# A two-stage Fourier mix on one core: the middle channel joined to channel 0, and the even-cosine product split by output parity

## The chip, the core and the metric

The kernel runs on one core of one Trainium2 chip. A core has five engines with a queue each: TensorE (PE; PEld are its weight loads), VectorE (DVE), ScalarE (ACT), GpSimd (POOL) and SyncE (SP, which here issues nearly all DMAs). Each works its own queue in order and waits on semaphores for the others. The metric is the time on the device in microseconds (us); lower is better.

## The reference

```python
# attention, for each of 8 batches and 8 heads; q, k, v are (8, 8, 576, 64), fp32
q_s = exp(q - max(q, -1)); q_s /= sum(q_s, -1) + 1e-9
k_s = exp(k - max(k, seq)); k_s /= sum(k_s, seq) + 1e-9
x = q_s @ (k_s.T @ v)                       # then (batch, 576, 8 * 64 = 512)

# Fourier mix and a two-layer MLP, for each batch
mixed = real(fft(fft(x, axis=1), axis=2))   # over 576 tokens, then over 512 channels
u = x + mixed
un = (u - mean(u, -1)) / sqrt(var(u, -1) + 1e-6)
out = u + relu(un @ w_ch1) @ w_ch2          # 512 x 2048 and 2048 x 512
```

## The kernel before

**Batches and order.** The eight batches follow each other, each in stages: attention, first Fourier stage (over tokens), second Fourier stage (over channels), normalisation, and the MLP's two layers (`up` and `down`, whose products are formed by Strassen's scheme; for batch 2 and later `down` goes two levels deep). The work is written as a list of steps with times, sorted by them once; each engine's queue is the order in which the steps issue. So attention and Fourier work of the next batch stand among the MLP products of the present one, at places fixed by hand. Batch 0 has an order of its own (`OPENING`); batch 1 is mixed into batch 0's plain MLP; batches 2 to 7 come from `timed`. The 64 tokens of a batch that don't fill a tile of 128 are shared: two batches form one tile together (`g`, and `mix_shared`).

**First Fourier stage.** The input is real, so only cosines and sines of folded inputs are needed. `folded` adds and subtracts mirrored tokens (`tokens_folded`), then mirrored channels (`columns_folded`, L1110), then token halves (`by_frequency`, L1123), and folds the channels once more (`columns_again`, L1129 and L1130): for each of four tiles `eo[i]`, L1129 writes the difference of mirrored channels and L1130, in place, their sum. They go over the tiles in the order 2, 3, 0, 1; tiles 2 and 3 feed the sines, 0 and 1 the cosines. `folds` (L1085 to L1088) does the same for the shared tokens' tile `g`. The order on DVE is that of the code: for tile 0 L1129, L1130, for tile 1 L1129, L1130, and then sums for the deep `down` (L1617). On POOL stand, at about the same time in batches 2 to 7, four sums of the last hidden tile (`a_side`, L405 to L408).

The products then take the tiles as stationary operands: five groups of channels k, each with an odd and an even half of the tokens (`blocks`, L1207): sines 2 and 3, then cosines 0, 1 and 4. Group 4 is one channel alone, the middle channel (number 128, `QD`) of the twice folded 128 (it is computed as 128 wide, of which one row is used). `tails` (L1234) adds the shared tokens. In batch 1 `block` (L1166, L1169) does the same, one group at a time. `copies` then lays the results out in SBUF by ACT: group k to `Z[:, k]` (L1246, "own") and, for the 64 shared rows, to `ZT[:, k]` (L1249, L1250); group 4 goes to row 0 of the tiles `Zr` and `ZTr`, whose other rows were set to zero at the start.

**Second Fourier stage.** `second` forms for each tile of 128 tokens one row of 512 outputs in PSUM: odd cosines from group 1, even cosines from group 0 (129 columns), sines from 2 and 3 (all on L1264). The middle channel's cosine is +1 for outputs of even number and -1 for odd ones; it is added to the even cosines by a product of its own (L1267), with `Zr` as 128 rows of which one is not zero and a row of signs as moving operand. ACT copies the sines (L1273), DVE forms sums and differences (L1281), and they are added to x. There are 20 such mixes: two own tiles in each of eight batches, and four shared ones.

All products are fp32; the profile lists each as two matmul records with a weight load each.

Of the kernel before, what the change touches and what calls it, by code (L numbers as in the profile page):

```python
# [43 lines left out]
ALU = mybir.AluOpType  # L44
AX = mybir.AxisListType

P = 128
B, H, S, DH = 8, 8, 576, 64
D = H * DH
# [9 lines left out]
Q = 32  # L59
# [79 lines left out]
class _Block:  # L139
# [906 lines left out]
    def t_times_kv(self, b):  # L1046
        nc, V = self.nc, self.nc.vector
        j, box = b % 2, []
        part = slice(W * j, W * j + W)

        F = lambda r: self.F[:, 2 * r + j]

        def times():
            box.extend(self.by_head(b, F, False, DH, shared=b != 1))
            px = box[-1]
            for a in range(2):
                for h in range(2):
                    for i in range(2):
                        n = HD + a * DH if b < 2 else FREE + (1 + a) * DH
                        t = box[2 + h] if b == 1 else px[-1][:, h]  # L1060
                        nc.tensor.matmul(t[64 * i:64 * i + 64, n:n + DH], lhsT=F(2 * i + a)[64 * h:64 * h + 64, P:],
                                         rhs=self.pairs[j][64 * h:64 * h + 64, 2 * i + a, 0:DH], start=True, stop=True)

        def copies():
            g = self.live["g", b] = self.halves()
            x = self.xshared(b // 2)[part]
            if b != 1:
                px = box.pop()
                for r, t in box:
# [12 lines left out]

        def folds():
            g = self.live["g", b]
            V.scalar_tensor_tensor(out=g[:, 1:HD], in0=g[:, D - 1:HD:-1], scalar=self.sign[:, 0:1], in1=g[:, 1:HD],  # L1085
                                   op0=ALU.mult, op1=ALU.add)
            V.tensor_tensor(out=g[:, NN:NN + QD], in0=g[:, 0:QD], in1=g[:, HD:QD:-1], op=ALU.subtract)
            V.tensor_tensor(out=g[:, 0:QD], in0=g[:, 0:QD], in1=g[:, HD:QD:-1], op=ALU.add)  # L1088

        return [(0, times), (1.3, copies), (8 if b > 1 else 3, folds)]  # L1090

    def folded(self, b):
# [30 lines left out]
        def columns_again(some):  # L1125

            for i in some:
                t, y = eo[i], eo[i][:, NN:]
                V.tensor_tensor(out=t[:, 0:QD], in0=y[:, 0:QD], in1=y[:, HD:QD:-1], op=ALU.subtract)  # L1129
                V.tensor_tensor(out=y[:, 0:QD], in0=y[:, 0:QD], in1=y[:, HD:QD:-1], op=ALU.add)  # L1130

        if b == 0:
            return tokens_folded, lambda some: (columns_parted if some[0] < 2 else columns_folded)(some), by_frequency, columns_again
# [12 lines left out]
    def block(self, b, k):  # L1146
        nc = self.nc
        box = []
        sines = k in (2, 3)
        own = slice(*{0: (NN, NN + QD), 4: (NN + QD, NN + QD + 1), 1: (0, QD), 2: (NN + 1, NN + QD + 1),  # L1150
                      3: (1, QD)}[k])
        tail = slice(*{0: (0, QD), 4: (QD, QD + 1), 1: (NN, NN + QD), 2: (1, QD + 1), 3: (NN + 1, NN + QD)}[k])
        n = own.stop - own.start
        if k == KT:

            own, tail = slice(own.start, own.start + P), slice(tail.start, tail.start + P)

        def times():
            eo, g = self.eo[b], self.live["g", b]
            if b not in self.Z:  # L1160
                self.Z[b] = self.work.tile([P, KT, HD], F32, tag="Z", name="Z", bufs=1)
            full = self.acc((own.stop - own.start, 512))
            f = sines * NM
            for odd, at, size in ((1, 0, MO), (0, MO, ME)):
                t = eo[3 - odd if sines else odd]
                nc.tensor.matmul(full[:, at:at + size], lhsT=t[:, own], rhs=self.ft[:, f + at:f + at + size], start=at == 0,  # L1166
                                 stop=False, skip_group_check=True)
            f += 2 * NM
            nc.tensor.matmul(full[:, 0:NM], lhsT=g[:, tail], rhs=self.ft[:, f:f + NM], start=False, stop=True,  # L1169
                             skip_group_check=True)  # L1170
            box.append(full[0:n])

        def copies():
            pz, Z = box.pop(), self.Z[b]
            z, zt = (self.Zr[0:1], self.ZTr[0:1]) if k == KT else (Z[0:n, k, :], self.ZT[0:n, k, :])
            nc.scalar.copy(paired(z), interleaved(pz[:, NT - 1:NT - 1 + 2 * ME])[:, 0:P, :])

            at = W * (b % 2)
            nc.scalar.mul(paired(zt[:, at:at + Q]), interleaved(pz[:, 0:2 * MO])[:, 0:NT - 1, ::-1],
                          -1.0 if sines else 1.0)  # L1180
            nc.scalar.copy(paired(zt[:, at + Q:at + W]), interleaved(pz[:, 0:2 * ME])[:, NT - 2::-1, ::-1])

        return [(0, times), (1.4, copies)]

    def blocks(self, b):

        nc = self.nc
        box = {}
        eo = self.eo.setdefault(b, {})
        cols = {0: (NN, 0), 1: (0, NN), 2: (NN + 1, 1), 3: (1, NN + 1), 4: (NN + QD, QD)}  # L1190
        wide = lambda k, i: slice(cols[k][i], cols[k][i] + (QD - 1 if k == 3 else P))
        place = lambda k, odd: slice((0, 1, 0, 1, 2)[k] * (ME - odd), (0, 1, 0, 1, 2)[k] * (ME - odd) + ME - odd)
        bank = lambda k, odd: box[k in (2, 3)][:QD - 1 if k == 3 else P, 1 - odd, place(k, odd)]
# [41 lines left out]
                                     start=first.get(k, False), stop=True, skip_group_check=True)  # L1235

        def copies(k, part, copy=nc.scalar.copy):
            n, sines, Z = {3: QD - 1, 4: 1}.get(k, P), k in (2, 3), self.Z[b]
            z, zt = (self.Zr[0:1], self.ZTr[0:1]) if k == KT else (Z[0:n, k, :], self.ZT[0:n, k, :])
            flat = box[sines][0:n].rearrange("p a n -> p (a n)")  # L1240
            odd, even = place(k, 1).start, D + place(k, 0).start

            def both(x, y, size, step=1):
                return bass.AP(flat.tensor, flat.offset + x, [flat.ap[0], [step, size], [y - x, 2]])
            if part == "own":
                copy(paired(z), both(odd + NT - 1, even + NT, P))  # L1246
                return
            w = W * (b % 2)
            nc.scalar.mul(paired(zt[:, w:w + Q]), both(even, odd, NT - 1), -1.0 if sines else 1.0)  # L1249
            nc.scalar.copy(paired(zt[:, w + Q:w + W]), both(even + NT - 1, odd + NT - 2, NT - 1, -1))  # L1250

        return own, tails, copies, early, sine

    def second(self, z, zr, adds, two=True, apart=None):

        nc, V = self.nc, self.nc.vector
        cd, box = self.cd, []
# [1 line left out]
        def times():  # L1259
            banks = apart() if apart else [self.acc((P, D), two)] * 2  # L1260
            parts = (1, 0, QD), (0, QD, QD + 1), (2, NN + QD - 1, QD), (3, NN, QD - 1)
            for k, at, size in (parts[2], (3, HD, QD), *parts[:2]) if apart else parts:
                rows, pm = QD - 1 if k == 3 else P, banks[k > 1]
                nc.tensor.matmul(pm[:, at:at + size], lhsT=z(k)[0:rows], rhs=cd[0:rows, at:at + size], start=True,  # L1264
                                 stop=(k != 0))
                if k == 0:
                    nc.tensor.matmul(pm[:, at:at + size], lhsT=zr(), rhs=cd[:, D:], start=False, stop=True)  # L1267
            box.extend(banks)

        def copy():  # L1270
# [30 lines left out]
    def mix_own(self, b, c):  # L1301
# [5 lines left out]
            t = self.two()  # L1307
            return [t[:, 0, :], t[:, 1, :]]

        return self.second(lambda k: self.Z[b][:, k, s], lambda: self.Zr[:, s], adds, apart=None if b else apart)  # L1310

    def norm(self, g):

# [520 lines left out]
def kernel(ctx: ExitStack, tc: tile.TileContext, q, kT, v, w1, w2, ft,  # L1834
# [69 lines left out]
        steps += at(dt, converted(i))  # L1904
    for p, dt in enumerate((15, 20, 25, 36, 41, 46.5, 83.5, 87)):
        steps += at(first + dt, combined(0, p))
    steps += [(t + 0.5 + 0.1 * i, lambda i=i: fetch(i)) for i in LATE_WORDS]
    steps.append((t + 6, lambda: setattr(blk, "spare_words", blk.raws[LATE_WORDS[0]].bitcast(F32))))
    steps += [(t + dt, lambda i=i: blk.load(i)) for i, dt in ((1, 14), (0, 36), (2, 40))] + [(t + 71, lambda: blk.load(3))]
# [32 lines left out]
def tables():  # L1942
# [15 lines left out]
    d, n = np.arange(P), np.arange(QD)  # L1958
    cd = np.zeros((P, 5 * QD + 1), np.float32)
    cd[:, :QD] = np.cos(turn(d, 2 * n + 1, D))  # L1960
    cd[:, QD:NN] = np.cos(turn(d, 2 * np.arange(QD + 1), D))
    cd[:QD - 1, NN:NN + QD - 1] = np.sin(turn(d[1:], 2 * n[1:], D))
    cd[:, NN + QD - 1:D] = np.sin(turn(d + 1, 2 * n + 1, D))
    cd[:, D:] = 1.0 - 2.0 * (np.arange(QD + 1) % 2)
# [29 lines left out]
```

## Time and profile before

| | |
|---|---|
| median of 3 runs | 1006.58 us (1006.44 to 1006.77) |
| profiled execution, span | 1006.6 us |
| PE busy | 995.6 us (99%) |
| DVE busy | 718.6 us (71%) |
| ACT busy | 493.2 us (49%) |
| POOL busy | 442.9 us (44%) |
| granted TensorE clock, mean | 1.000 |

The profiled execution's own time is its span; it stands on the median of the runs. A row of the timeline gives the start in us from the span's start, the length in us, the engine, the line of the kernel, the operation, what it writes and reads, its shape, and how many instructions are merged in it; in brackets, the idle time of the engine before it and what ended that. A row of a line's own view gives the shortest, the median and the longest duration in ns, the first and the last start in us, and the shapes. L with a number is a line of the kernel before, if nothing else is said.

### The profile page before, as it was taken

What the parts mean: (1) busy time and instruction counts of PE and PEld (TensorE: products, weight loads), DVE (VectorE), ACT (ScalarE), POOL (GpSimd) and SP (SyncE); (2) the same over time, 40 slices, a digit from 0 to 9 for tenths busy, and PEclk for the clock granted to TensorE, in tenths of its full rate; (3) what the DMA queues carried; (4) which work ended last, traced back from release to release, by engine and by line L of the source; (5) the groups of instructions that cost most, each with busy time, mean ns of one, the idle gap of its engine ahead of it and who ended that gap; (6) DMA issues with size and microseconds to landing.
All of it is one profiled execution on the core that took longest, in us unless ns stands there. A gap on an engine that the chain in (4) does not pass through costs nothing.

```text
span 1006.6 us, 19808 instructions
## 1 busy us (share of the span) xinstructions
PE 995.6 (99%) x7562; PEld 855.7 (85%) x7562; DVE 718.6 (71%) x1356; ACT 493.2 (49%) x1277; POOL 442.9 (44%) x445
## 2 busy tenths in 40 slices
PE   8999999999999999999999999999999999999998
PEld 6844464888888899889988998899889998998897
DVE  6898898666765887588756877688667945685563
ACT  4585642872468228832775177625772342151200
POOL 4263420357535637664655465655646450040000
PEclk9999999999999999999999999999999999999999
DMA  9987499687989666975677577847753765674573
GB/s 300 258 281 245 158 240 346 205 243 226 342 283 272 230 230 219 266 237 210 251 220 242 206 269 237 253 174 270 231 204 135 267 213 200 224 265 172 183 256 132
DMA packets 123559, 236.37 MB, mean 235 GB/s; under 512 B 24184, under 2 KB 88440, under 8 KB 112840
## 3 DMA queue, kind: packets, MB, share of 16 engines
q1 hardware_dynamic: 123096, 234.58, 71.0%
q8 instruction: 60, 0.98, 0.4%
q14 instruction: 35, 0.29, 0.1%
q10 hardware_dynamic: 288, 0.26, 0.1%
q0 software_dynamic: 80, 0.26, 0.1%
HBM read 199.94 MB, written 39.06 MB: 237 GB/s over the span
## 4 chain that ended last, share of the span: by engine, by line
PE 87%; DVE 7%; ACT 3%; DMA 1%; issue 1%; SPq 0%; POOL 0%; DVEq 0%; POOLq 0%
PE bb L1544 16%; PE ba L1544 11%; PE bc L1544 11%; PE bb L1671 10%; PE ba L1671 7%; PE bc L1671 7%; PE bb L1641 5%; PE bc L1479 2%; PE bb L1760 2%; PE two L840 2%; PE one L755 2%; PE two L1207 1%; PE two L1264 1%; PE ba L1479 1%; PE bc L1760 1%; PE ba L1760 1%
## 5 line engine op out<-in xcount | busy, mean ns | idle before, releaser
L1544 PE MATMUL bb<-unT,big 128*128 128x256 f32 x768 | 183.3, 380 | 0.0
L1544 PEld LDWEIGHTS bb<-unT,big 128*128 128x128 f32 x768 | 144.8, 190 | 20.7 <-DVE u L1514 0.7
L1556 ACT ACTIVATE big<-big 128x512 f32<-128x512 f32 x96 | 59.8, 629 | 147.6 <-DVE big L1555 141.0
L1544 PE MATMUL ba<-unT,big 128*128 128x256 f32 x512 | 123.9, 382 | 0.0
L1544 PE MATMUL bc<-unT,big 128*128 128x256 f32 x512 | 121.5, 380 | 0.1
L817 ACT ACTIVATE qT<-q 32x128 f32<-32x128 f32 x384 | 117.9, 307 | 5.9 <-DVE q L807 0.8
L1544 PEld LDWEIGHTS bc<-unT,big 128*128 128x128 f32 x512 | 96.9, 190 | 13.7 <-DVE big L1555 0.5
L1544 PEld LDWEIGHTS ba<-unT,big 128*128 128x128 f32 x512 | 95.5, 190 | 13.9 <-issue 0.5
L1514 DVE TENSOR_TENSOR u<-bb,s 128x512 f32<-128x512 f32 x66 | 45.2, 685 | 85.0 <-PE bb L1544 66.5
L1671 PE MATMUL bb<-big 128*128 128x128 f32 x848 | 103.8, 276 | 0.2 <-DVE u L1678 0.2
L1671 PEld LDWEIGHTS bb<-big 128*128 128x128 f32 x848 | 98.9, 192 | 1.0 <-DVE u L1678 1.0
L1390 POOL COPY unT<-unT 32x256 f32<-32x256 f32 x98 | 42.0, 428 | 90.2 <-DVE unT L1382 85.9
L1621 POOL TENSOR_TENSOR x<-x,big 128x512 f32<-128x512 f32 x45 | 60.9, 1368 | 46.0 <-DVE big L1678 19.7
L1617 DVE TENSOR_TENSOR big<-big 128x512 f32<-128x512 f32 x98 | 79.9, 842 | 0.0
L1671 PE MATMUL ba<-big 128*128 128x128 f32 x640 | 79.0, 276 | 0.0
L1671 PEld LDWEIGHTS ba<-big 128*128 128x128 f32 x640 | 75.0, 192 | 0.8
L1390 ACT COPY unT<-unT 32x256 f32<-32x256 f32 x126 | 50.7, 402 | 31.3 <-DVE unT L1382 29.5
L804 POOL TENSOR_TENSOR q<-q,qm 128x512 f32<-128x512 f32 x24 | 25.8, 1073 | 88.2 <-DVE qm L799 53.1
L405 POOL TENSOR_TENSOR big<-big 128x512 f32<-128x512 f32 x24 | 30.4, 1268 | 68.4 <-ACT big L1556 68.4
L1641 PE MATMUL bb<-big 128*128 128x256 f32 x256 | 58.3, 379 | 0.0
L1555 DVE TENSOR_TENSOR big<-bc,u 128x512 f32<-128x512 f32 x64 | 44.0, 688 | 17.3 <-PE bc L1544 16.4
L1641 PEld LDWEIGHTS bb<-big 128*128 128x128 f32 x256 | 48.0, 190 | 6.1
(336 smaller groups left out, 1917.9 us busy)
## 6 DMA issues: line engine op xcount, KB each, us to landing
big<-w2d SPq DMA_DIRECT2D x67, 1024.0 KB, 4.6
big<-w1s SPq DMA_DIRECT2D x64, 896.0 KB, 4.7
big<-w2s SPq DMA_DIRECT2D x16, 1024.0 KB, 4.8
big<-in_w_dram SPq DMA_DIRECT2D x21, 512.0 KB, 6.0
w2d<-big SPq DMA_DIRECT2D x42, 256.0 KB, 6.5
kb<-in_kT_dram SPq DMA_DIRECT2D x28, 320.0 KB, 7.8
q<-in_q_dram SPq DMA_DIRECT2D x28, 256.0 KB, 6.0
vt<-in_v_dram SPq DMA_DIRECT2D x84, 80.0 KB, 2.7
```

What stands on the lines that cost most here:

```text
L405: e1.tensor_tensor(out=to(4), in0=at(2), in1=at(3), op=ALU.add)
L817: nc.scalar.activation(to[t, i * Q:i * Q + Q], one, ACT.Exp)
L1390: copy(to, of)
L1514: plus = lambda t: V.tensor_tensor(out=temp(t), in0=box["bb"][:], in1=box["s1"][:], op=ALU.add)
L1544: nc.tensor.matmul(bank()[:, i, :], lhsT=w[:, WA_AT[m], k * P:(k + 1) * P], rhs=self.unT[g][:, B_AT[m], k, :], start=first and i == 0 and ...
L1555: steps = [(0, lambda: V.tensor_tensor(out=hp(i), in0=bank()[:], in1=u()[:], op=ALU.add)), (0.8, lambda: nc.scalar.activation(hp(i), hp(i) ...
L1556: (0.8, lambda: nc.scalar.activation(hp(i), hp(i), ACT.Relu))]
L1617: e.tensor_tensor(out=to(o), in0=to(x), in1=to(y), op=op)
L1621: E.tensor_tensor(out=x, in0=x, in1=tile(m), op=ALU.add)
L1641: nc.tensor.matmul(box[name][:, i, :], lhsT=h[p][:, A_AT[m], i * P:(i + 1) * P], rhs=self.stream[n][:, p, :], start=p == 0 and (m != 1 or ...
L1671: nc.tensor.matmul(box[place[n]][:, i, :], lhsT=own(m)(A_AT[n])[:, f, :], rhs=w[:, r // 2, r % 2 * P:r % 2 * P + P], start=first and f == ...
L1760: nc.tensor.matmul(bank()[:, i, :], lhsT=h[p][:, A_AT[m], i * P:(i + 1) * P], rhs=w[:, p, :], start=first and i == 0 and p == 0, stop=p == ...
```

## The change

For batches 1 to 7, in the tiles eo[0], eo[1] and `g` (the cosine side), the middle channel and channel 0 are replaced by their sum and their difference: new `ends_folded`, two DVE operations on one column each, behind L1130 of tiles 0 and 1 and behind L1088. Group 4 of the first stage now computes the difference. The cosine of channel 0 is 1 everywhere and that of the middle channel alternates, so the even outputs of the even-cosine part need only the sum and the odd outputs only the difference, with the other 127 channels in both. `Zr` and `ZTr` therefore become whole copies of group 0's result in which row 0 is the difference: ACT copies group 0 to both places (`places`), and group 4 over row 0. The second stage multiplies `Z[:, 0]` for the 65 even outputs and `Zr` for the 64 odd ones; the columns of the table `cd` are sorted by parity, and the result is written to every second column of PSUM. The product with the row of signs is gone.

Batch 0 keeps the old form for its own two mixes (`alone`): its part is 65 and 64 columns with `Z`, and then the 129 columns of the row of signs. Its shared tokens are joined afterwards by four POOL operations (`ends_shared`), since they share a tile with batch 1's.

```diff
@@ folds (shared tokens g)
             V.tensor_tensor(out=g[:, 0:QD], in0=g[:, 0:QD], in1=g[:, HD:QD:-1], op=ALU.add)
+            if b:
+                self.ends_folded(g)
...
+    def ends_folded(self, y):
+        V = self.nc.vector
+        V.tensor_tensor(out=y[:, QD + 1:QD + 2], in0=y[:, 0:1], in1=y[:, QD:QD + 1], op=ALU.subtract)
+        V.tensor_tensor(out=y[:, 0:1], in0=y[:, 0:1], in1=y[:, QD:QD + 1], op=ALU.add)
@@ columns_again
                 V.tensor_tensor(out=y[:, 0:QD], in0=y[:, 0:QD], in1=y[:, HD:QD:-1], op=ALU.add)
+                if b and i < 2:
+                    self.ends_folded(y)
@@ block (batch 1), and alike in blocks
-        own = slice(*{0: (NN, NN + QD), 4: (NN + QD, NN + QD + 1), 1: (0, QD), 2: (NN + 1, NN + QD + 1),
+        own = slice(*{0: (NN, NN + QD), 4: (NN + QD + 1, NN + QD + 2), 1: (0, QD), 2: (NN + 1, NN + QD + 1),
...
+    def places(self, b, k, n):
+        some = [] if k == KT else [(self.Z[b][0:n, k, :], self.ZT[0:n, k, :])]
+        if k in (0, KT) and (b or k):
+            some.append((self.Zr[0:n], self.ZTr[0:n]))
+        return some
+
+    def ends_shared(self):
+        G, z, zr = self.nc.gpsimd, self.ZT[:, 0, 0:W], self.ZTr[:, 0:W]
+        less = self.ZTr[0:1, W:P]
+        G.tensor_tensor(out=less, in0=z[0:1], in1=zr[0:1], op=ALU.subtract)
+        G.tensor_tensor(out=z[0:1], in0=z[0:1], in1=zr[0:1], op=ALU.add)
+        G.tensor_copy(zr, z)
+        G.tensor_copy(zr[0:1], less)
@@ copies (blocks; alike in block)
-            z, zt = (self.Zr[0:1], self.ZTr[0:1]) if k == KT else (Z[0:n, k, :], self.ZT[0:n, k, :])
...
+            for z, zt in self.places(b, k, n):
+                if part == "own":
+                    copy(paired(z), both(odd + NT - 1, even + NT, P))
+                    continue
+                nc.scalar.mul(paired(zt[:, w:w + Q]), both(even, odd, NT - 1), -1.0 if sines else 1.0)
+                nc.scalar.copy(paired(zt[:, w + Q:w + W]), both(even + NT - 1, odd + NT - 2, NT - 1, -1))
@@ second
-                nc.tensor.matmul(pm[:, at:at + size], lhsT=z(k)[0:rows], rhs=cd[0:rows, at:at + size], start=True,
-                                 stop=(k != 0))
-                if k == 0:
-                    nc.tensor.matmul(pm[:, at:at + size], lhsT=zr(), rhs=cd[:, D:], start=False, stop=True)
+                if k:
+                    nc.tensor.matmul(pm[:, at:at + size], lhsT=z(k)[0:rows], rhs=cd[0:rows, at:at + size], start=True,
+                                     stop=True)
+                    continue
+                for odd in range(2):
+                    nc.tensor.matmul(pm[:, at + odd:at + size:2], lhsT=z(0) if alone or not odd else zr(),
+                                     rhs=cd[:, at + W * odd + odd:at + W + odd * W + 1], start=True, stop=not alone,
+                                     skip_group_check=True)
+                if alone:
+                    nc.tensor.matmul(pm[:, at:at + size], lhsT=zr(), rhs=cd[:, D:], start=False, stop=True,
+                                     skip_group_check=True)
@@ mix_own
-        return self.second(lambda k: self.Z[b][:, k, s], lambda: self.Zr[:, s], adds, apart=None if b else apart)
+        return self.second(lambda k: self.Z[b][:, k, s], lambda: self.Zr[:, s], adds, apart=None if b else apart, alone=not b)
@@ the list of steps, batch 0's first MLP layer
+    steps.append((first + 24.3, blk.ends_shared))
@@ tables
-    cd[:, QD:NN] = np.cos(turn(d, 2 * np.arange(QD + 1), D))
+    cd[:, QD:NN] = np.cos(turn(d, 2 * np.concatenate([np.arange(0, QD + 1, 2), np.arange(1, QD, 2)]), D))
```

More of the change, by code (lines that the diff above doesn't have):

```diff
@@ L1149, in block @@
         sines = k in (2, 3)
-        own = slice(*{0: (NN, NN + QD), 4: (NN + QD, NN + QD + 1), 1: (0, QD), 2: (NN + 1, NN + QD + 1),
+        own = slice(*{0: (NN, NN + QD), 4: (NN + QD + 1, NN + QD + 2), 1: (0, QD), 2: (NN + 1, NN + QD + 1),
                       3: (1, QD)}[k])
-        tail = slice(*{0: (0, QD), 4: (QD, QD + 1), 1: (NN, NN + QD), 2: (1, QD + 1), 3: (NN + 1, NN + QD)}[k])
+        tail = slice(*{0: (0, QD), 4: (QD + 1, QD + 2), 1: (NN, NN + QD), 2: (1, QD + 1), 3: (NN + 1, NN + QD)}[k])
         n = own.stop - own.start
@@ L1174, in copies @@
             pz, Z = box.pop(), self.Z[b]
-            z, zt = (self.Zr[0:1], self.ZTr[0:1]) if k == KT else (Z[0:n, k, :], self.ZT[0:n, k, :])
-            nc.scalar.copy(paired(z), interleaved(pz[:, NT - 1:NT - 1 + 2 * ME])[:, 0:P, :])
             at = W * (b % 2)
-            nc.scalar.mul(paired(zt[:, at:at + Q]), interleaved(pz[:, 0:2 * MO])[:, 0:NT - 1, ::-1],
-                          -1.0 if sines else 1.0)
-            nc.scalar.copy(paired(zt[:, at + Q:at + W]), interleaved(pz[:, 0:2 * ME])[:, NT - 2::-1, ::-1])
-        return [(0, times), (1.4, copies)]
+            for z, zt in self.places(b, k, n):
+                nc.scalar.copy(paired(z), interleaved(pz[:, NT - 1:NT - 1 + 2 * ME])[:, 0:P, :])
+                nc.scalar.mul(paired(zt[:, at:at + Q]), interleaved(pz[:, 0:2 * MO])[:, 0:NT - 1, ::-1],
+                              -1.0 if sines else 1.0)
+                nc.scalar.copy(paired(zt[:, at + Q:at + W]), interleaved(pz[:, 0:2 * ME])[:, NT - 2::-1, ::-1])
+        return [(0, times), (1.4, copies)]
+    def places(self, b, k, n):
[10 more added lines that the diff above has]
+        G.tensor_copy(zr[0:1], less)
     def blocks(self, b):
@@ L1189, in blocks @@
         eo = self.eo.setdefault(b, {})
-        cols = {0: (NN, 0), 1: (0, NN), 2: (NN + 1, 1), 3: (1, NN + 1), 4: (NN + QD, QD)}
+        cols = {0: (NN, 0), 1: (0, NN), 2: (NN + 1, 1), 3: (1, NN + 1), 4: (NN + QD + 1, QD + 1) if b else (NN + QD, QD)}
         wide = lambda k, i: slice(cols[k][i], cols[k][i] + (QD - 1 if k == 3 else P))
@@ L1237, in copies @@
         def copies(k, part, copy=nc.scalar.copy):
-            n, sines, Z = {3: QD - 1, 4: 1}.get(k, P), k in (2, 3), self.Z[b]
-            z, zt = (self.Zr[0:1], self.ZTr[0:1]) if k == KT else (Z[0:n, k, :], self.ZT[0:n, k, :])
+            n, sines = {3: QD - 1, 4: 1}.get(k, P), k in (2, 3)
             flat = box[sines][0:n].rearrange("p a n -> p (a n)")
@@ L1244, in both, with second @@
                 return bass.AP(flat.tensor, flat.offset + x, [flat.ap[0], [step, size], [y - x, 2]])
-            if part == "own":
-                copy(paired(z), both(odd + NT - 1, even + NT, P))
-                return
             w = W * (b % 2)
-            nc.scalar.mul(paired(zt[:, w:w + Q]), both(even, odd, NT - 1), -1.0 if sines else 1.0)
-            nc.scalar.copy(paired(zt[:, w + Q:w + W]), both(even + NT - 1, odd + NT - 2, NT - 1, -1))
+            for z, zt in self.places(b, k, n):
+                if part == "own":
[3 more added lines that the diff above has]
+                nc.scalar.copy(paired(zt[:, w + Q:w + W]), both(even + NT - 1, odd + NT - 2, NT - 1, -1))
         return own, tails, copies, early, sine
-    def second(self, z, zr, adds, two=True, apart=None):
+    def second(self, z, zr, adds, two=True, apart=None, alone=False):
         nc, V = self.nc, self.nc.vector
```

## The prediction

> **What bounds the kernel now.** I read the page first, then the groups by line for the products that change, then the timeline of one stage after another around them.
>
> ```profile
> span 1006.6 us, 19808 instructions
> ...
> PE 995.6 (99%) x7562; PEld 855.7 (85%) x7562; DVE 718.6 (71%) x1356; ACT 493.2 (49%) x1277; POOL 442.9 (44%) x445
> ...
> PE 87%; DVE 7%; ACT 3%; DMA 1%; issue 1%; SPq 0%; POOL 0%; DVEq 0%; POOLq 0%
> ```
>
> PE is busy 99% of the span and carries 87% of the chain that ended last. So whatever PE's queue gains or waits after the opening goes to the end almost one to one. The profiled span, 1006.6 us, stands on the median of the runs (1006.58), so the sum is made against 1006.6.
>
> **The product that is split.** One mix of the last batch, on PE's timeline:
>
> ```profile
> 779.18 0.61 PE L1264 MATMUL two<-cd,Z 128*128 128x128 f32 x4
> 779.63 0.39 PE L1267 MATMUL two<-cd,Zr 128*128 128x129 f32 x2
> 779.85 0.61 PE L1264 MATMUL two<-cd,Z 128*128 128x128 f32 x4
> 780.30 1.06 PE L1671 MATMUL bc<-big,unT 128*128 128x128 f32 x8
> ```
>
> Every fp32 product is two records, each with its own weight load. Ten records take 780.30 - 779.18 = 1.12 us, 0.112 each. There are 20 mixes. In 18 of them (all but batch 0's two) the even-cosine part had four records of 129 columns, and gets two of 65 and two of 64: half the columns, as many records. If the columns set the pace, this gives back 18 x 4 x 0.056 = 4.0 us. If the loads do, it gives nothing. One place in the trace decides it: the warming product of 64 columns in the opening, with the same 128x128 weights.
>
> ```profile
> 8.79 0.33 PE L270 MATMUL two<-pairs 128*128 128x64 f32 x2
> 8.68 0.30 PEld L270 LDWEIGHTS two<-pairs 128*128 128x128 f32 x2
> L270 PE MATMUL two<-pairs x26: 222/380/793, 1.2 to 12.4; 128*128 128x256 f32 x22, 128*128 128x64 f32 x4
> L1267 PEld LDWEIGHTS two<-cd,Zr x26: 192/192/192, 35.9 to 784.3; 128*128 128x128 f32 x26
> L755 PEld LDWEIGHTS one<-vt,kb x360: 132/138/138, 184.9 to 726.3; 128*64 128x64 f32 x180
> ```
>
> A record of 64 columns lasts 0.222 alone (the minimum); two take 0.33 from first start to last end, so the second ran 0.11 behind the first, though it has half the columns. Its load is also 0.30 - 0.19 = 0.11 behind the first load. And a load of 64 weight columns is 192 - 138 = 54 ns shorter than one of 128: 0.84 ns a column, 108 ns for 128. So 64 columns are no faster than 128 behind a full load. I take 0.109 a record: 72 x 0.003 = **-0.2 us**, with 0 and -4.0 as ends; the end near 0 is the one whose row has this very shape. The Trainium skill ("TensorE: Matmul & The Clock Gate", section LDWEIGHTS) states that a load costs its column count over 1.2 ns, whatever the rows, which by its figure is 107 ns here and would leave nothing of the saving either. By that rule, the trace agrees.
>
> **Batch 0, opening.** There channel 0 and the middle channel are not joined: the part becomes 65, 64 and the old 129 columns, so each of two mixes gets two records more, 4 x 0.112 = 0.45 us on PE.
>
> ```profile
> 36.24 4.48 PE L270 MATMUL tr<-pairs 128*128 128x256 f32 x20
> 40.74 0.52 PE L1365 MATMUL tr<-ident,eo 128*128 128x128 f32 x3
> ```
>
> The 20 warming records behind them end at 40.72, the first turn starts at 40.74. It waits for them, which move by 0.45, and for DVE's normalisation, which follows the first mix and moves by 0.22. I take **+0.3 us** (0.2 if DVE's side decides, 0.45 if PE's).
>
> **DVE's new operations.** For each batch from 1 on, six operations on one column: two on the shared tokens' `g`, and two each on eo[0] and eo[1] after L1130. A small operation with two inputs in SBUF costs 0.16 us (L1343's minimum, below), and DVE leaves 0.03 us before an operation that needs the one ahead. The two on `g` take 2 x (0.16 + 0.03) = 0.38 us and fall where DVE then idles for PE, here 0.39 in the last batch:
>
> ```profile
> 747.77 0.69 DVE L1555 TENSOR_TENSOR big<-bb,s 128x512 f32<-128x512 f32 x1 [0.39 <-PE bb L1544]
> ```
>
> They are costed at 0; were that cover gone, 0.4 us a batch, 2.7 for seven. The four on eo are another matter. Batch 3, DVE, POOL and PE:
>
> ```profile
> 341.24 1.27 POOL L405 TENSOR_TENSOR big<-big 128x512 f32<-128x512 f32 x1 [3.38 <-ACT big L1556]
> 341.33 1.32 DVE L1130 TENSOR_TENSOR eo<-eo 128x128 f32<-128x128 f32 x1
> 342.58 0.28 DVE L1129 TENSOR_TENSOR eo<-eo 128x128 f32<-128x128 f32 x1
> 342.59 1.40 POOL L406 TENSOR_TENSOR big<-big 128x512 f32<-128x512 f32 x1
> 342.89 1.25 DVE L1130 TENSOR_TENSOR eo<-eo 128x128 f32<-128x128 f32 x1
> 343.95 1.31 POOL L407 TENSOR_TENSOR big<-big 128x512 f32<-128x512 f32 x1
> 344.06 1.75 DVE L1617 TENSOR_TENSOR unT<-big 128x512 f32<-128x512 f32 x1
> 345.34 1.60 POOL L408 TENSOR_TENSOR big<-big 128x512 f32<-128x512 f32 x1
> 345.77 1.15 PE L1207 MATMUL two<-ft,eo 128*128 128x144 f32 x8
> L1130 DVE TENSOR_TENSOR eo<-eo x30: 293/294/1399, 30.9 to 766.0; 128x128 f32<-128x128 f32 x30
> ```
>
> L1130 takes 0.29 us, but here 1.32 and 1.25: it starts inside a POOL operation and ends 0.15 after that ends, twice. While POOL runs its four sums back to back, DVE gets one operation through per POOL operation, and a second only if it starts before POOL's next. PE's L1207 at 345.77 is the first product that reads eo[0] and eo[1]; now eo[1] is ready at 344.14, 1.63 us ahead. Do operations on one or two columns wait too?
>
> ```profile
> 389.88 1.27 POOL L1396 TENSOR_TENSOR unT<-unT 128x512 f32<-128x512 f32 x1 [1.18 <-DVE km L720]
> 390.79 0.39 DVE L720 TENSOR_TENSOR km<-km,across 128x16 f32<-128x16 f32 x1 [0.57 <-ACT across L716]
> L720 DVE TENSOR_TENSOR km<-km,across x14: 161/173/465, 66.3 to 707.5; 128x16 f32<-128x16 f32 x14
> L1343 DVE SCALAR_TENSOR_TENSOR mv<-mv,std x15: 161/164/1036, 159.2 to 888.4; 128x2 f32<-128x2 f32 x14, 128x4 f32<-128x4 f32 x1
> ```
>
> They do: L720's 16 columns end at 391.18, 0.03 behind POOL's end at 391.15, and L1343's 2 columns took 1.04 instead of 0.16 at worst. The Trainium skill ("SBUF — State Buffer", section Who interferes with whom) states that a DVE instruction with two SBUF inputs and a GpSimd one that reads SBUF exclude each other whole, the first to issue going first. By that rule, the trace agrees.
>
> So I play batch 3 on, calling subtract and add of eo[i] s_i and a_i. Through the first L1130 (done 342.65) nothing changes. s0 needs its output and issues at 342.68, behind L406 (342.59), which now has no DVE operation in front and ends at 343.86 by 1.27, the length that batch 2's undisturbed operations show:
>
> ```profile
> 234.70 1.27 POOL L406 TENSOR_TENSOR big<-big 128x512 f32<-128x512 f32 x1
> 235.93 1.27 POOL L407 TENSOR_TENSOR big<-big 128x512 f32<-128x512 f32 x1
> 238.52 0.66 PE L1207 MATMUL two<-ft,eo 128*128 128x144 f32 x4
> ```
>
> s0 ends at 343.88. a0 issues at 343.91, behind L407, which as now starts 0.04 before L406 ends: 343.82 to 345.09; a0 ends at 345.11. The second L1129 needs none of these and starts at 345.04, ahead of L408 (345.17, 0.08 after L407), done at 345.32; L408, held up 0.13, ends at 346.57. The second L1130 issues at 345.35, loses to L408, ends at 346.72. POOL's next operation comes of a product that stands behind L1207 on PE, so s1 and a1 run free: 346.75 to 346.91, 346.94 to 347.10. With 0.04 to PE, L1207 starts at 347.14 instead of 345.77: PE idles 1.37 us. If s0 and a0 slip through together, it is 1.2; if L1129 loses as well, 1.5. The last batch repeats the pattern, as do the three between:
>
> ```profile
> 764.31 1.27 POOL L405 TENSOR_TENSOR big<-big 128x512 f32<-128x512 f32 x1 [3.39 <-ACT big L1556]
> 768.84 1.15 PE L1207 MATMUL two<-ft,eo 128*128 128x144 f32 x8
> ```
>
> L405 to L1207 is 4.53 us in both. Five batches (3 to 7): **+6.8 us** (6.0 to 7.5). In batch 2 PE comes at 238.52, later against POOL's sums: 0 to 0.25, I take 0. In batch 1 POOL is not at these sums: 0. DVE's next work, L1617, starts up to 3 us late, but meets no POOL operation then, and PE reads its sums only in the products behind the first mix: 0.
>
> **ACT's new copies.** Channel block 0 is copied twice: one 128x256 copy more, and one pair more for the shared tokens.
>
> ```profile
> 349.91 1.20 ACT L1246 COPY Z<-two 128x256 f32<-128x256 f32 x4 [0.57 <-PE two L1234]
> 351.48 0.16 ACT L1250 COPY ZT<-two 127x32 f32<-127x32 f32 x1
> 351.63 0.16 ACT L1250 COPY ZT<-two 128x32 f32<-128x32 f32 x1
> 351.89 0.61 PE L1264 MATMUL two<-cd,Z 128*128 128x128 f32 x4
> 774.85 0.16 ACT L1250 COPY ZT<-two 128x32 f32<-128x32 f32 x1
> 775.06 0.71 PE L1264 MATMUL two<-cd,ZT 128*128 128x128 f32 x4
> ```
>
> A big copy moves ACT's queue by (1.20 - 0.37)/3 = 0.28, a pair by 0.15. In batches 3 to 6 the first mix takes the bank that the sines' last copy frees at 351.64; PE comes at 351.89, 0.25 later. 0.28 late plus 0.04 to PE costs 0.07 each, 0.3 in all. In the last batch the shared mix is first and needs the copy that ends at 775.01, 0.05 ahead; 0.43 late costs 0.4. Together **+0.7 us** (0 to 1.4: none, or a whole big copy, in each of the five). POOL's four small operations for batch 0's shared tokens stand between weight conversions in PE's dense first layer: 0 (to 1).
>
> **Sum.** -0.2 + 0.3 + 6.8 + 0.7 = +7.6: 1006.6 + 7.6 = **1014.2 us**. About 0.2%, 2 us, is what a measurement of this kernel can tell from no change.
>
> **Rivals.**
> *The columns set PE's pace and the DVE wait comes too:* 1014.2 - 3.8 = 1010.4. Against it stands the 64-column row, one place only. Chance 0.06.
> *DVE's small operations hide:* the waits of 1.37 are not there, since the one-column operations get through between two POOL operations or POOL's sums come at another moment; 1014.2 - 6.8 = 1007.4, no change. For it speaks that no row shows a single column; against it L1343. Chance 0.11.
> *Faster:* both, 1007.4 - 3.8 = 1003.6. It decides from the point where the column saving (4.0) exceeds the waits. The Trainium skill (the same TensorE page, section Back-to-back issue gap) gives the gap of an isolated matmul by its columns alone, which would be this rival. Chance 0.05. That the change doesn't save columns at all can't be: the list of instructions has the 65 and 64.
> *Worse:* the shifted order on DVE brings further meetings with POOL in the mixes or in batch 2, another 2 to 4 us: 1016 to 1018. Chance 0.08.
>
> **How the numbers follow.** The forecast has 0.70. Its own terms run from -0.2 + 0.2 + 6.0 + 0 = 6.0 to 0 + 0.45 + 7.5 + 0.25 + 1.4 + 1 = 10.6, so 1012.6 to 1017.2, the upper end only with all at their worst. Reaching down to the first rival and up into the last, the range is 1010.0 to 1017.0, with some 0.8 inside. Slower by over 0.2%: 0.70 + 0.06 + 0.08 = 0.84; within 0.11; faster 0.05.
>
> **What would show it.** In the profile after: ten records of a mix still take about 1.1 us; PE idles some 1.4 us before the cosine group's first product in batches 3 to 7, released by DVE's one-column add; that add starts after POOL's last sum. I am wrong if the 65-column records follow each other in 0.06, or if the one-column operations last 0.16 amid POOL's sums and PE doesn't wait.

## The result, and the profile after

| | before | after |
|---|---|---|
| median | 1006.67 us (4 runs, 1006.44 to 1007.23) | 1016.55 us (4 runs, 1015.58 to 1017.25) |
| ratio | | 1.0097, 95% interval 1.0083 to 1.0112 |
| the same in a later comparison (e9) | 1007.03 us (11 runs) | 1015.83 us (5 runs) |
| ratio | | 1.0087, 95% interval 1.0073 to 1.0101 |
| profiled span | 1006.6 us | 1014.4 us |

The change makes the kernel slower by 9.9 us in the first comparison and by 8.8 us in the second. The two profiled spans differ by less, 7.8. A run takes 1.7 to 2.4 us more than its span wherever both are known, so the execution of before that was profiled would have taken about 1008.4 (its own time isn't on record), not the median: the spans of 59 later runs of before have their median at 1005.3. Some of that is in the opening (see e8).

The page of the changed kernel, its span, the engines' busy time and the chain that ended last:

```profile
span 1014.4 us, 19884 instructions
...
PE 996.7 (98%) x7566; PEld 855.7 (84%) x7566; DVE 723.1 (71%) x1398; ACT 496.0 (49%) x1298; POOL 438.3 (43%) x449
...
PE 79%; DVE 12%; ACT 4%; DMA 3%; issue 1%; POOL 1%; SPq 1%; POOLq 0%; ACTq 0%; DVEq 0%
```

PE is busy for 1.1 us more than before, hardly anything. But DVE now stands for 12% of the chain that ended last; it had 7%. PE's list of waits says which wait that is (the line that waits and its releaser; then us in total, times, longest):

```profile
PE two L1232 <- DVE eo L1098: 5.8, 5, 1.2
PE tr L985 <- DVE q L957: 0.8, 1, 0.8
```

The first row is new: five times, once in each of the batches 3 to 7, PE stands 1.2 us before the cosine products (L1232, in the kernel before L1207) until DVE's one-column add (L1098) is done. The timeline of batch 3, the stage that the prediction played through:

```profile
341.16 1.27 POOL L405 TENSOR_TENSOR big<-big 128x512 f32<-128x512 f32 x1 [3.37 <-ACT big L1588]
341.25 1.33 DVE L1138 TENSOR_TENSOR eo<-eo 128x128 f32<-128x128 f32 x1
342.51 1.27 POOL L406 TENSOR_TENSOR big<-big 128x512 f32<-128x512 f32 x1
342.61 1.18 DVE L1097 TENSOR_TENSOR eo<-eo 128x1 f32<-128x1 f32 x1
343.73 1.27 POOL L407 TENSOR_TENSOR big<-big 128x512 f32<-128x512 f32 x1
343.82 1.19 DVE L1098 TENSOR_TENSOR eo<-eo 128x1 f32<-128x1 f32 x1
344.94 0.28 DVE L1137 TENSOR_TENSOR eo<-eo 128x128 f32<-128x128 f32 x1
345.08 1.26 POOL L408 TENSOR_TENSOR big<-big 128x512 f32<-128x512 f32 x1
345.25 1.24 DVE L1138 TENSOR_TENSOR eo<-eo 128x128 f32<-128x128 f32 x1
346.52 0.16 DVE L1097 TENSOR_TENSOR eo<-eo 128x1 f32<-128x1 f32 x1
346.72 0.16 DVE L1098 TENSOR_TENSOR eo<-eo 128x1 f32<-128x1 f32 x1
346.99 1.03 PEld L1232 LDWEIGHTS two<-ft,eo 128*128 128x128 f32 x8 [1.54 <-POOL big L408]
347.02 1.22 PE L1232 MATMUL two<-ft,eo 128*128 128x144 f32 x8 [1.17 <-DVE eo L1098]
```

One column takes 1.18 and 1.19 us here, and 0.16 once POOL is through its four sums. Each dependent operation lets one POOL operation pass. L405 to L1232 is now 347.02 - 341.16 = 5.86 us, and was 4.53: PE comes 1.33 later. That is more than the 1.17 of idle time, since in the kernel before this product started 0.16 ahead of the end of the one before it (345.77 against 345.93), and behind the wait it doesn't. The operations stand in the order of the prediction, and its times are met to within 0.25 us.

And one mix of the last batch, with the even-cosine product in halves (L1294):

```profile
787.00 0.39 PE L1290 MATMUL two<-cd,Z 128*128 128x128 f32 x2
787.22 0.33 PE L1294 MATMUL two<-cd,Z 128*128 128x65 f32 x2
787.39 0.39 PE L1294 MATMUL two<-cd,Zr 128*128 128x64 f32 x2
787.61 0.66 PE L1290 MATMUL two<-cd,Z 128*128 128x128 f32 x4
788.11 0.72 PE L1703 MATMUL bc<-big,unT 128*128 128x128 f32 x5
```

From the first start to that of the product behind the mix (L1703) it is 788.11 - 787.00 = 1.11 us for ten records; before it was 1.12. Half the columns bought 0.01 us at most.

### The profile page after: what moved, and what is told of

Read it like the earlier page. It is cut to its first block, busy times and chain, and to the rows that moved or that the text cites. A ratio compares the mean times of both kernels' runs of the same rounds, so it can differ in the third digit from the quotient of the medians.

```text
span 1014.4 us, 19884 instructions
## 1 busy us (share of the span) xinstructions
PE 996.7 (98%) x7566; PEld 855.7 (84%) x7566; DVE 723.1 (71%) x1398; ACT 496.0 (49%) x1298; POOL 438.3 (43%) x449
## 4 chain that ended last, share of the span: by engine, by line
PE 79%; DVE 12%; ACT 4%; DMA 3%; issue 1%; POOL 1%; SPq 1%; POOLq 0%; ACTq 0%; DVEq 0%
PE bb L1576 15%; PE ba L1576 10%; PE bb L1703 10%; PE bc L1576 9%; PE bc L1703 7%; PE ba L1703 7%; PE bb L1673 3%; PE bc L1511 2%; DVE eo L1138 2%; ACT qT L817 2%; PE two L840 2%; PE one L755 1%; PE bb L1792 1%; PE ba L1511 1%; PE ba L1792 1%
## 5 line engine op out<-in xcount | busy, mean ns | idle before, releaser
L817 ACT ACTIVATE qT<-q 32x128 f32<-32x128 f32 x384 | 117.9, 307 | 5.9 <-DVE q L807 0.7
L1703 PE MATMUL bb<-big 128*128 128x128 f32 x848 | 103.8, 276 | 0.3 <-DVE u L1710 0.2
L1703 PEld LDWEIGHTS bb<-big 128*128 128x128 f32 x848 | 98.9, 192 | 1.0 <-DVE u L1710 1.0
L1703 PE MATMUL ba<-big 128*128 128x128 f32 x640 | 79.0, 276 | 0.0
L1703 PEld LDWEIGHTS ba<-big 128*128 128x128 f32 x640 | 75.0, 192 | 0.8
L1649 DVE TENSOR_TENSOR big<-big 128x512 f32<-128x512 f32 x98 | 75.7, 801 | 0.0
L405 POOL TENSOR_TENSOR big<-big 128x512 f32<-128x512 f32 x24 | 30.5, 1269 | 68.4 <-ACT big L1588 68.4
L1587 DVE TENSOR_TENSOR big<-bc,u 128x512 f32<-128x512 f32 x64 | 44.1, 688 | 17.2 <-PE bc L1576 16.4
```

Source lines behind the costliest of these rows:

```text
L405: e1.tensor_tensor(out=to(4), in0=at(2), in1=at(3), op=ALU.add)
L817: nc.scalar.activation(to[t, i * Q:i * Q + Q], one, ACT.Exp)
L1587: steps = [(0, lambda: V.tensor_tensor(out=hp(i), in0=bank()[:], in1=u()[:], op=ALU.add)), (0.8, lambda: nc.scalar.activation(hp(i), hp(i) ...
L1649: e.tensor_tensor(out=to(o), in0=to(x), in1=to(y), op=op)
L1703: nc.tensor.matmul(box[place[n]][:, i, :], lhsT=own(m)(A_AT[n])[:, f, :], rhs=w[:, r // 2, r % 2 * P:r % 2 * P + P], start=first and f == ...
```

## The experiments

All are timed against the kernel before in the same rounds; before's medians there were 1007.02 (e1 to e4), 1006.97 (e5 to e8) and 1007.03 us (e9, e10).

**e1: the chain of small operations alone, on the kernel before.**

```diff
                 V.tensor_tensor(out=y[:, 0:QD], in0=y[:, 0:QD], in1=y[:, HD:QD:-1], op=ALU.add)
+                if b and i < 2:
+                    spare = y[:, QD + 1:QD + 2]
+                    V.tensor_tensor(out=spare, in0=y[:, 0:1], in1=y[:, QD:QD + 1], op=ALU.subtract)
+                    V.tensor_tensor(out=spare, in0=spare, in1=y[:, QD:QD + 1], op=ALU.add)
```

> The kernel before, with two one-column operations on VectorE behind each of the two column sums of eo[0] and eo[1] in batches 1 to 7 (the second reads what the first wrote; both write a spare column, so the arithmetic is the one of before). Products, copies and the operations on g are those of before. Theory A (the dependent one-column operations let POOL's sums pass one by one, and TensorE waits 1.3 to 1.4 us in five batches): 1006.6 + 5 x 1.35 = 1013.4 us, 1012.6 to 1014.2, and TensorE waits for the second one-column operation in batches 3 to 7. Rival B (the products in two halves and the copies made twice cost the time): within 1 us of before, 1006.6 to 1007.5.

Measured: 1012.56 us, 1.0056 (1.0042 to 1.0070), 5.5 us over before, with no product or copy changed. The size was missed: 5 x 1.35 = 6.8 over before was expected, some 1.2 too much, and the time lies just under the lower end of 1012.6. PE's waits and the last steps of batch 3 say why:

```profile
PE two L1211 <- DVE eo L1130: 3.9, 5, 0.8
...
343.87 1.24 DVE L1130 TENSOR_TENSOR eo<-eo 128x128 f32<-128x128 f32 x1
345.14 0.16 DVE L1133 TENSOR_TENSOR eo<-eo 128x1 f32<-128x1 f32 x1
345.26 1.22 PE L1211 MATMUL two<-ft,eo 128*128 128x144 f32 x8 [0.78 <-DVE eo L1130]
```

PE's first cosine product doesn't read the spare column. It is released by L1130 (345.11), not by the second small operation (345.34 to 345.50), so it comes some 0.4 us earlier than in the changed kernel. That L1130 itself starts only amid POOL's last sum (L408, 343.70), where in the kernel before it started amid the second (L406), is the chain's doing: nothing else was added. So the chain makes the wait on its own, five times.

**e2, e3, e4: the chain taken away, moved to another engine, moved in time.** e2 drops the call in `columns_again`; e3 puts it on ACT:

```diff
                 if b and i < 2:
-                    self.ends_folded(y)
+                    ends = y[:, 0:1], y[:, QD:QD + 1]
+                    nc.scalar.activation(out=y[:, QD + 1:QD + 2], in_=ends[1], func=ACT.Identity, bias=ends[0], scale=-1.0)
+                    nc.scalar.activation(out=ends[0], in_=ends[1], func=ACT.Identity, bias=ends[0], scale=1.0)
```

e4 leaves it on DVE and moves the step of tiles 0 and 1 ahead of the work that starts POOL's sums:

```diff
-... (2, 6.5, 6.5, 6, 6), (3, 9, 9, 12, 12)), (
+... (2, 6.5, 6.5, 6, 6), (3, 9, 9, 9.2, 9.2)), (
```

> The changed kernel without the four one-column operations on eo[0] and eo[1]; it leaves out the joining of the two channels in the spectrum of all batches but the first, so its output isn't the reference's. Products, copies and the operations on g stay. Theory A: the waits of 1.33 us in five batches go, 1016.5 - 7 = 1009.5 us or less; what is left above the 1006.6 of before is the price of products, copies and opening, forecast at 0.8. Rival B: it stays at 1015 to 1017. If the columns had saved their 4.0 us behind the waits, it would come out at 1003 to 1004.

> The changed kernel with the four one-column operations on eo[0] and eo[1] made by ScalarE (Identity with the other column as bias), which is idle there and shares no port with POOL's sums. Theory A: as without the operations, plus their time on ScalarE where TensorE is already waiting for nothing: 1009.5 us, 1008 to 1010.5. If any dependent operation at this place costs the wait, whatever its engine: 1015 to 1017.

> The changed kernel with the last step of folding eo[0] and eo[1] (and with it the four one-column operations) due at 9.2 instead of 12 in batches 3 to 7, so that VectorE does it ahead of the L1587 whose activation starts POOL's four sums. The operations are the same, on the same engine. Theory A: amid no POOL work they last 0.16 each and TensorE finds its tiles ready: the waits of 1.33 us go, 1009.5 us, with up to 5 x 0.3 more if the L1587, 1.6 us later, is missed further on. Rival C (the longer chain on VectorE itself is too long, whatever POOL does): 1015 to 1016.

| | median | ratio to before |
|---|---|---|
| e2, left out | 1008.56 us | 1.0016 (1.0006 to 1.0025) |
| e3, on ACT | 1008.96 us | 1.0021 (1.0011 to 1.0030) |
| e4, earlier on DVE | 1009.09 us | 1.0018 (1.0009 to 1.0027) |

All three lose the waits, and they are equal within their intervals, so it doesn't matter how the meeting is avoided. e3 on its timeline, batch 3:

```profile
342.02 1.40 POOL L406 TENSOR_TENSOR big<-big 128x512 f32<-128x512 f32 x1
342.19 0.29 ACT L1141 ACTIVATE eo<-eo 128x1 f32<-128x1 f32 x1 [1.59 <-DVE eo L1138]
```

On ACT one column takes 0.29 us in the middle of a POOL operation. In e4 the same two DVE operations stand ahead of POOL's sums and take 0.16 each (the later L1587 costs nothing that can be seen):

```profile
342.28 0.16 DVE L1097 TENSOR_TENSOR eo<-eo 128x1 f32<-128x1 f32 x1
342.47 0.16 DVE L1098 TENSOR_TENSOR eo<-eo 128x1 f32<-128x1 f32 x1
...
343.98 1.59 POOL L405 TENSOR_TENSOR big<-big 128x512 f32<-128x512 f32 x1 [5.16 <-ACT big L1588]
```

So neither the engine alone nor the length of the chain makes the wait, but DVE and POOL at the same moment. What is left, 1.5 to 2.1 us over before, is what the rest of the change costs.

**e5 and e6: what sets the pace of the products.** Both build on e3. e5 multiplies all 129 columns by `Z` and by `Zr`, in the same four records; e6 gives the second product 32 weight columns and 64 moving ones.

```diff
-                    nc.tensor.matmul(pm[:, at + odd:at + size:2], lhsT=z(0) if alone or not odd else zr(),
-                                     rhs=cd[:, at + W * odd + odd:at + W + odd * W + 1], ...)
+e5                  nc.tensor.matmul(pm[:, at:at + size], lhsT=zr() if odd else z(0), rhs=cd[:, at:at + size], ...)
+e6, odd             nc.tensor.matmul(pm[0:32, at + 1:at + size:2], lhsT=zr()[:, 0:32], rhs=cd[:, at:at + QD:2], ...)
```

> The kernel with the joining on ScalarE (e3), with all 129 columns in both even-cosine products of batches 1 to 7 in place of 65 and 64: as many records and loads, twice the columns; it leaves out the parting of the outputs, so its output isn't the reference's. Theory A (the weight loads set the pace, 0.109 to 0.112 us a record): 72 x 0.003 = 0.2 us more than e3, which stood at 1.0021 of before, so 1.0015 to 1.0030 of before, and ten records of a mix still take about 1.1 us. Rival (the columns set it): 4.0 us more, 1.006 of before.

> As e5, but the second even-cosine product has 32 weight columns in place of 128 and 64 moving columns in place of 129 (it leaves out most of that product, so its output isn't the reference's); the number of products and records stays. If the load of the weights is what a record waits for (0.84 ns a weight column), 32 of them load in 0.027 us and its two records fall to what 64 moving columns take, about 0.056 each: 36 x 0.056 = 2.0 us less than e5, and the ten records of a mix take 1.0 us instead of 1.1. If every record has a floor of 0.11 us whatever its weights: as e5.

e5 measured 1008.76 us, 1.0017 (1.0008 to 1.0026), against e3's 1.0021, and its mix takes 1.12 us: twice the columns cost nothing that can be measured. The rival, 1.006, is out. e6 measured 1011.69 us, 1.0045 (1.0031 to 1.0059): slower than e5 by 2.9, where I expected a gain of 2.0 or nothing. Its mix shows why:

```profile
358.73 0.39 PE L1305 MATMUL two<-cd,Z 128*128 128x129 f32 x2
359.04 0.14 PEld L1302 LDWEIGHTS two<-cd,Zr 128*32 128x32 f32 x2
359.05 0.30 PE L1302 MATMUL two<-cd,Zr 128*32 128x64 f32 x2
359.28 0.71 PE L1292 MATMUL two<-cd,Z 128*128 128x128 f32 x4
```

The narrow records start 0.32 after the wide ones (in e5 0.23), and the next wide ones 0.23 after the narrow. In e5 each load starts 0.11 ahead of its product (356.94 and 357.05 for the second half); here the loads at both changes of shape start with theirs, 0.01 ahead (359.04, and 359.27 for the wide ones behind). So going from one shape of weights to another and back costs more than the narrow pair saves, 0.2 us a mix over e5, and e6 doesn't answer its question. Rows of the kernel before bear on it. Its products with 64 weight columns and 65 moving ones stand many in a row, and so do others with 128 weight columns and 256 moving ones:

```profile
184.37 0.80 PE L755 MATMUL one<-vt,Z 128*64 128x65 f32 x20
185.00 0.75 PE L755 MATMUL one<-vt,kb 128*64 128x65 f32 x20
...
759.22 1.89 PE L1544 MATMUL bb<-unT,big 128*128 128x256 f32 x8
```

Twenty records take 0.63 us from one row to the next. They start two at a time (one writes rows 0 to 63 of the output, the other rows 64 to 127), one pair every 0.058 us. With 65 columns and half the weights, a pair takes half the time of one record with 65 columns and all the weights (787.22 above). With 256 columns and all the weights, eight records take 1.73 us (the next eight start at 760.95), 0.216 each, 0.84 ns a column. All this fits a record that waits for the longer of its load and its columns, each at about 0.84 ns a column, so that at 128 weights and 128 columns the two are equal. That reading rests on traces; no run varied the load alone.

**e7: without the second copies.** On e3, `places` gives group 0 to `Z` only.

```diff
-        if k in (0, KT) and (b or k):
+        if k == KT:
```

> The kernel with the joining on ScalarE (e3), without the second copy of channel block 0 into the other tile (one 128x256 copy, and one pair for the shared tokens, in batches 1 to 7); it leaves out that part, so its output isn't the reference's. Theory A: the start of the first mix in batches 3 to 6 comes 0.16 us earlier (0.06 of waiting for ScalarE and 0.10 in which the next weights load), the last batch's shared mix 0.4: 0.8 to 1.0 us less than e3 in the trace, 1.0012 of before. Rival (the copies are hidden and what is left of e3 over before lies in the opening): the same as e3, 1.0021.

Measured 1008.62 us, 1.0018 (1.0009 to 1.0027): against e3 0.3 less, too little for the measured times to tell. The traces tell it. The first mix of batch 3, in the changed kernel and then in e7:

```profile
353.07 0.16 ACT L1275 COPY ZT<-two 127x32 f32<-127x32 f32 x1
353.28 0.30 PEld L1290 LDWEIGHTS two<-cd,Z 128*128 128x128 f32 x2
353.28 0.49 PE L1290 MATMUL two<-cd,Z 128*128 128x128 f32 x2
353.61 0.34 PE L1294 MATMUL two<-cd,Z 128*128 128x65 f32 x2
```

```profile
351.34 0.30 PEld L1292 LDWEIGHTS two<-cd,Z 128*128 128x128 f32 x2
351.45 0.39 PE L1292 MATMUL two<-cd,Z 128*128 128x128 f32 x2
351.67 0.33 PE L1296 MATMUL two<-cd,Z 128*128 128x65 f32 x2
```

In the changed kernel PE waits for the bank until ACT's last copy of the sines ends (353.23), about 0.06 us. The load that in e7 runs 0.11 ahead of its product starts with it, so the two records take 0.33 in place of 0.22. Each of the four batches 3 to 6 loses 0.16 so, and the last batch's shared mix 0.2 (its first product 0.43 late, 0.27 of which comes back within the mix). None of this is left in e7. So the copies cost 4 x 0.16 + 0.2 = about 0.85 us, by the traces.

**e8: the kernel before, once more.**

> The kernel before, for a second profiled execution beside these. Expected: a span 1.5 to 2.5 us under its time, as in the runs of the others, and an opening (the first 100 us) that differs by some tenths of a us up to 1.5 us from that of the first profile, which shows how much of a difference between two single profiles the opening makes by itself.

1008.85 us, a span of 1007.1. From 22 us on its starts stand at +0.5, at 111 us at -0.3 against those of the first profile. Later a single wait adds 0.7. In the first 22 us the two are up to 0.9 apart. So two executions of one kernel differ by that much within the opening, and e1, which changes nothing there, stood at -1.5 at 111 us.

**e9 and e10: the whole against its parts, and the two operations on `g`.** e9 is the changed kernel; e10 makes all of `ends_folded` on ACT.

> The changed kernel once more, timed in the same rounds as e10, so that the whole can be set against the sum of its parts: five waits of 1.33 us with 0.08 of weight loading behind each (7.0), ScalarE's second copies (0.16 in four batches and 0.2 in the last, 0.85), the opening (0.3 for batch 0's two more products), batch 1's key work 0.4 late behind the two operations on g, 0.3 at a changed meeting of VectorE and GpSimd in batch 2: 8.8 us over before, 1.0088. If something is still missing from the list, it comes out at 1.010 again.

> As e3, with the two one-column operations on g of every batch on ScalarE too. The trace of e3 has them on VectorE at 106.05 to 106.41 in batch 1, ahead of the weight conversion and the query work that TensorE waits for at 110.2 (0.91 us there, 0.5 in the kernel before). If they are what makes that wait longer, it falls back to about 0.5 and the span by 0.4 us: about 1008.6 us, 1.0017 of before. If it doesn't shrink, the wait comes of something else, and the time is that of e3, 1.0021.

e9: 1015.83 us, 1.0087 (1.0073 to 1.0101), 8.8 us over before, the sum of the list. e10: 1009.69 us, 1.0029 (1.0018 to 1.0041), not less than e3 but 0.7 more, within what the intervals leave open. Its trace confirms that the two operations hold DVE up, but there is no gain. DVE's query work in batch 1 (L957) and the product that waits for it, in before, in the changed kernel and in e10:

```profile
110.48 0.69 DVE L957 TENSOR_TENSOR q<-q,qrec 128x512 f32<-128x512 f32 x1
111.23 0.44 PE L985 MATMUL tr<-ident,q 128*128 128x128 f32 x2 [0.52 <-DVE q L957]
```

```profile
106.41 0.16 DVE L1097 TENSOR_TENSOR eo<-eo 128x1 f32<-128x1 f32 x1
106.60 0.16 DVE L1098 TENSOR_TENSOR eo<-eo 128x1 f32<-128x1 f32 x1
106.68 0.69 DVE L391 TENSOR_SCALAR big<-acc 128x512 int32<-128x512 int32 x1
109.82 0.69 DVE L957 TENSOR_TENSOR q<-q,qrec 128x512 f32<-128x512 f32 x1
110.57 0.66 PE L985 MATMUL tr<-ident,q 128*128 128x128 f32 x4 [0.79 <-DVE q L957]
```

```profile
109.31 0.69 DVE L957 TENSOR_TENSOR q<-q,qrec 128x512 f32<-128x512 f32 x1
110.06 0.66 PE L985 MATMUL tr<-ident,q 128*128 128x128 f32 x4
```

From the last sum on `g` (L1088, which starts at 107.13, 106.08 and 105.96 in the three) to L957 DVE takes 3.35 us in before, 3.74 with the two operations and 3.35 again without them: they cost 0.39 there. In e10 the wait is wholly gone, 0.8 us less than in e3, but only in part for this reason: PE itself reaches this place 0.65 us later than in e3, since that execution was 0.8 behind e3's already after the opening. Further on the operations stand on ACT ahead of copies (L817) that the query products (L840) read; these slip by 0.14 to 0.39 us in each of four batches, and other waits take the rest.

## Why the prediction was right

It gave 1014.2 us and a range of 1010.0 to 1017.0; both measurements, 1016.55 and 1015.83, lie in it, above the middle, the first of them not far from the upper end. The slowdown of 7.6 that it forecast is 1.2 short of e9 and 2.3 short of the first comparison. Point by point:

- **Products, -0.2 (0 to -4.0): right.** Nothing of the 4.0 appeared: 1.11 us for ten records, and e5 with all columns is as fast. The 64-column row of the opening, one place only, was the right witness.
- **Batch 0's opening, +0.3: right.** Each of its two mixes is 0.22 longer in the trace (0.17 and 0.05), and 0.27 of the 0.44 are left when the turns begin (L1365, now L1397), in the changed kernel's two traces and alike in e2 to e7 and e10. The measured times can't tell it: e8 moves by more.
- **The wait for DVE, +6.8 (6.0 to 7.5): right in place, count, cause and size.** Five waits of 1.33 us in place of 1.37, none in batches 1 and 2. That it is so near has some luck in it: DVE was done 0.22 earlier than I played it (346.88), and from there to PE's start it took 0.14 where I had put 0.04. I had missed a small part: behind each wait the next load isn't done yet, 0.08 more (its load at 346.99 is 0.03 ahead of the product; in before it was 0.21 ahead). 5 x 1.41 = 7.0 in all.
- **`g`'s two operations, 0: wrong in batch 1.** I took their cover from the last batch (0.39 us of idle DVE). In batch 1 DVE isn't idle behind them: L391 starts 0.08 after L1098 has started, and PE waits at L985 0.79 us in place of 0.52. In the eight traces that have these operations on DVE (the changed kernel twice, e2 to e7), PE loses 0.27 to 0.42 there. The price that I gave for missing cover, 0.4 a batch, was right; the cover should have been looked up in each batch.
- **ACT's copies, +0.7: near in size by luck, wrong in parts.** Batches 3 to 6 cost 0.16 each and not 0.07, since a wait of 0.06 leaves 0.10 of loading uncovered; the last batch costs 0.2 and not 0.4, since 0.27 comes back. The two errors offset each other: 0.85 in all.
- **POOL's four operations: 0, as forecast**; no wait for them is in PE's list.
- **Not in the sum: a changed meeting in batch 2, +0.3.** Before, DVE's L1579 ran first and took 0.65 us; after, POOL's half of the same sum runs first, DVE's (L1611) takes 1.50, and the work behind it reaches PE 0.3 late at 290 us. The same step shows in all of e2 to e7 and e10, and not in e1 and e8. So it doesn't hang on the operations on eo (e2), the halved columns (e5), the second copies (e7) or DVE's operations on `g` (e10) alone; why POOL comes first there stays open. It is of the kind of the last rival, but far smaller.

```profile
273.01 1.80 POOL L1579 TENSOR_TENSOR big<-big 128x512 f32<-128x512 f32 x1 [1.61 <-DMA big<-w1s]
273.02 0.65 DVE L1579 TENSOR_TENSOR big<-big 128x512 f32<-128x512 f32 x1
```

```profile
272.35 1.27 POOL L1611 TENSOR_TENSOR big<-big 128x512 f32<-128x512 f32 x1 [1.30 <-DVE big L1611]
272.66 1.50 DVE L1611 TENSOR_TENSOR big<-big 128x512 f32<-128x512 f32 x1
```

The parts as the traces have them: 0.27 + 7.0 + 0.35 + 0.85 + 0.3 = 8.8, against 8.8 in e9 (7.4 to 10.2), and 9.9 in the first comparison, whose interval reaches from 8.4 to 11.3. Intervals of that width bear out the 7.0, not the small parts, which rest on the traces. One premise was wrong without doing harm: the profiled execution of before didn't stand on the median, since a run is longer than its span. The sum is a difference and was added to a number that happened to be the median.

No version came out below the kernel before. As long as the weights stay 128 wide there is nothing for the joining to win (e5), and narrower ones would mean a change of shape twice in each mix, which cost 0.2 us a mix in e6. That no other form of it is faster is argued, not shown.

## What to carry to other kernels

Before columns are cut from a product, look whether its records wait for the columns or for the load: find a row with fewer columns behind the same weights. The price of a chain of tiny operations can lie in what another engine runs at that moment and not in its length: here 0.16 us became 1.18 each, amid GpSimd's sums. And cover that is found in one stage has to be found in every stage where the operation stands.

## What the runs showed of the hardware that was not expected

- A wait of TensorE costs more than itself: the load for the record behind it no longer runs ahead, which cost 0.08 us behind each of the five waits and 0.10 in the first mixes of batches 3 to 6.
- Going between weights of 128 and of 32 columns and back costs TensorE time: the load at each change starts with its product and not 0.11 us ahead, and the mix is 0.2 us longer (e6). Records with 64 weight columns run in pairs side by side, one pair every 0.058 us.
- VectorE and GpSimd took turns: amid the four sums a VectorE operation that depends on the one ahead let a whole GpSimd operation pass even if it has one column (1.17 to 1.19 us, twice in each of batches 3 to 7), while the next independent one gets through behind it (L1137 at 344.94, 0.28). The Trainium skill ("SBUF — State Buffer", section Who interferes with whom) lists ScalarE with ports of its own. By that rule, the trace agrees: 0.29 us in e3 under a running GpSimd operation.
